# Second batch's pooled loads behind the first batch's x, with a planner that counts 270 GB/s

## The chip, the core and the metric

The kernel runs on one core of a Trainium2 chip. The metric is the device time of one execution in microseconds (us): the median of three runs before the change is 971.7 us (968.58 to 975.79). The engines are named as in the profile: PE is TensorE's matrix product, PEld its weight load, DVE is VectorE, ACT is ScalarE, POOL is GpSimd, and SP is SyncE, which here issues every DMA.

## What is computed

Eight batches of eight heads, 576 positions of 64 elements each. Every head has two attentions whose sum is taken: a pooled one, over groups of four positions (144 pooled positions), and a local one, in which a position sees the three on either side of it. The sum, laid out as 4608 tokens of 512 elements, goes through a feed-forward network (FFN) with 2048 hidden elements and a leaky ReLU.

```python
q_d = q.reshape(B, H, Sd, factor, D).mean(axis=3)          # k_d and v_d likewise, factor = 4
out_up = np.repeat(sm_attn(q_d, k_d, v_d), factor, axis=2)
mask = np.abs(pos[:, None] - pos[None, :]) < factor
scores = np.where(mask, scale * np.matmul(q, k.transpose(0, 1, 3, 2)), -1e9)
attn_out = out_up + np.matmul(softmax(scores), v)
h = x @ w_in                                               # x: attn_out as 4608 x 512
out = np.maximum(0.01 * h, h) @ w_out
```

## The kernel before, in words

The tokens go through the FFN in thirteen chunks: chunks 0 and 1 are the first batch (256 and 320 tokens), then 256, 320 and nine of 384 tokens. Each product in float32 is made of three in a shorter form: x, the hidden values and both weights are each split in a high and a low part (xh and xl, gh and gl, wih and wil, woh and wol). The up product of a chunk and one f (128 hidden elements; f goes from 0 to 15) is twelve matmuls into a bank "hp" (L698); ACT and DVE turn it into gh and gl (L708, L709, L711); the down product is twelve matmuls into four banks acc0 to acc3 (L738). Chunks 0 and 1 go through in two passes each, f 0 to 7 and then f 8 to 15; the second pass loads the stored half output again (L749 to L763) and adds to it. In all this is 4992 matmuls; the texts number them from 0, and chunk 2 begins with number 768.

Weights are made on the chip. `convert(f, k)` loads w_in (k = 0) or w_out (k = 1) of one f into a buffer of 512 KB, copies a part on ACT into a "head" tile (L266), shifts and joins on DVE (L268), casts the high part on ACT or DVE (L279, L276) and subtracts on POOL for the low part (L281). The buffer is free again after the subtraction. For the load it may take any of the buffers k, v, prod (two) and up, and for the first f also xh1 and xl1, which chunk 1 needs later. Weights from f 8 on lie where the first batch's tiles lay, and so are cast only after that batch is done ("late").

The first batch (BANDED = 1) has its local attention on PE (`banded`: scores L453 and L461, transposes L488, value product L502, sums into x at L514 to L521), in two parts: blocks 0 to 3 of 64 positions are chunk 0, blocks 4 to 8 are chunk 1. For the other batches POOL multiplies and DVE adds up: `scores` (L560, L566) loads q and k tiles, `values` (L621, L627) a v tile, and `landing` transposes the result on PE (L658), adds the pooled part and splits it into xh and xl (L665 to L673).

The pooled attention of a batch comes in four units c (two heads each). `pooled` loads q and k as one tile of 576 KB ("qk", one buffer from the second batch on) and v ("vs"), adds groups of four on DVE or POOL (L338, L332, L334), takes scores on PE (L351), the exponential on ACT (L363), transposes (L390) and the value product (L402), and leaves the result in "outd". `widen` repeats it four times in "up" (L645) for the landing.

What runs when is planned while the program is written. Every piece of work is a task with a rank; class `Order` keeps, for each engine, the time at which it is free by its own table of costs (COST, HOP, and a data rate for the DMA wire at L172), and lets the task that can start first write its next instruction. On the chip, each engine then works off its instructions in just that order and waits at each for what it needs. SP does so too: a load behind a store that has nothing to store yet waits with it.

Of the kernel before, what the change touches and what calls it, by code (L numbers as in the profile page):

```python
# [25 lines left out]
NF, NE, NC = DF // 128, DM // 128, DM // 128  # L26
# [2 lines left out]
SIZES = (4, 5, 6, 6, 6, 6, 6, 6, 6, 6, 6)  # L29
QB = 48  # L30
FSPLIT = 8
BANDED = 1
WIN = 64 + W - 1
BLKS = ((0, 4), (4, 9))
# [39 lines left out]
OMAX = max(XMAX)  # L74
COST = {"ACT": (0.13, 0.00083), "DVE": (0.08, 0.00104), "POOL": (0.25, 0.00217)}
HOP = 0.2
SAFE = 0.4
SCARCE, HURRY = ("pt",), 1000

# [16 lines left out]
class Order:  # L96
# [51 lines left out]
    def run(self):  # L148
        while self.tasks:
            for task in sorted((t for t in self.tasks if t[3][0] != "op"), key=lambda t: t[:2]):  # L150
                got = self.grant(task)
                if got is not None:
                    self.resume(task, got)
                    break
            else:
                best = None
                for task in self.tasks:
                    if task[3][0] == "op":
                        _, eng, dur, ready, size = task[3][:5]
                        start = max(self.engine[eng], ready)  # L160
                        if size:
                            start = max(start, self.wire - 6.0)
                        key = (start, task[0], task[1])
                        if best is None or key < best[0]:
                            best = key, task
                assert best is not None, [t[3] for t in self.tasks]
                (start, _, _), task = best
                _, eng, dur, ready, size = task[3][:5]
                free = self.engine[eng]
                self.engine[eng] = start + dur  # L170
                if size:
                    self.wire = max(self.wire, start + 1.2) + size / 300e3  # L172
                    done = self.wire + 0.8
                else:
                    done = start + dur + HOP
                self.log.append((start, eng, dur, task[0], start - free, task[3][5:]))
                self.resume(task, done)
# [3 lines left out]
def attn_moe(ctx: ExitStack, tc, qkt, vd, qb, kb, vb, vwb, band, identb, w_in, w_out, ident, edge, out):  # L181
# [9 lines left out]
    od = Order(bufs)  # L191

    def slot(*tags):
        return (yield ("slot", tags, 0))
# [8 lines left out]
    def op(eng, n, *after, times=1):  # L203
        if eng == "PE":
            dur = n
        else:
            a, k = COST[eng]
            dur = times * a + k * n
        return (yield ("op", eng, dur, max((0.0,) + after), 0, after))
# [9 lines left out]
    def wait(name, n=1):  # L219
        return (yield ("wait", name, n))  # L220
# [30 lines left out]
        nc.vector.memset(h, 0)  # L251

    def convert(f, k):
        s = yield from slot("k", "v", "prod", "up", *(("xh1", "xl1") if f < 4 else ()))
        st = sb(s, [128, HALFS * (DM + 1)], U16)
        raw = st[:, 1:1 + HALFS * DM]
        if k == 0:
            t = yield from load(raw.rearrange("p (c m) -> p c m", c=NC), w_in_v[:, f], 524e3, s.t)
        else:
            t = yield from load(raw, w_out_v[:, f], 524e3, s.t)  # L260
        mid = st.bitcast(I32).rearrange("p (m w) -> p m w", w=2)[:, :DM, 1]
        top = st.rearrange("p (m h) -> p m h", h=HALFS)[:, 1:, 0].bitcast(BF16)
        s_u = yield from slot("head")
        head = heads[s_u.index % len(heads)]
        t = yield from op("ACT", 1500, t, s_u.t)
        nc.scalar.copy(out=head.bitcast(F16).rearrange("p (m h) -> p m h", h=2)[:, :, 1], in_=top)  # L266
        t = yield from op("DVE", 780, t)
        nc.vector.scalar_tensor_tensor(out=mid, in0=mid, scalar=13, in1=head, op0=ALU.logical_shift_right, op1=ALU.bitwise_or)  # L268
        s_u.free(t)
        tf = mid.bitcast(F32)  # L270
        if f >= FSPLIT:
            yield from wait("late")
        hi, lo = (w.rearrange("p c m -> p (c m)") for w in weight(f, k))
        if k:
            t = yield from op("DVE", 512, t)
            nc.vector.tensor_copy(out=hi, in_=tf)  # L276
        else:
            t = yield from op("ACT", 512, t)
            nc.scalar.copy(out=hi, in_=tf)  # L279
        t = yield from op("POOL", 590, t)  # L280
        nc.gpsimd.tensor_tensor(out=lo, in0=tf, in1=hi.bitcast(F32), op=ALU.subtract)  # L281
        s.free(t)
        od.signal(("w", f, k), t)
# [2 lines left out]
    xt = {}  # L286
    kept = {}

    def outd_tile(b):
        s = yield from slot("outd")  # L290
        outd[b] = sb(s, [128, NC, SD], F32)
        od.signal(("outd", b), s.t)
        t = yield from wait(("read", b), 8 if b < BANDED else 2 * len(PARTS[b]))
        s.free(t)
# [11 lines left out]
        s_l.free(t)  # L306

    def fetch(b, c, pool):
        if pool is None:
            sq, sv = (yield from slot(*(("qk", "up") if b < BANDED else ("qk",)))), (yield from slot("vs"))  # L310
            qk, vs = sb(sq, [128, 2, S], F32), sb(sv, [72, 2, 2, D, FAC], F32)
        else:
            sq, sv = None, (yield from slot("su_vs"))
            qk = pool.tile([128, 2, S], F32, name=f"qk{c}")
            vs = sb(sv, [72, 2, 2, D, FAC], F32, pool)
        tq = yield from load(qk, qkt[b, c], 590e3, sq.t if sq else 0.0)
        od.signal(("asked", b, c))
        kept[b, c] = qk
        od.signal(("qk", b, c), tq)
        tv = yield from load(vs, vd[b, c], 295e3, sv.t if sv else 0.0)  # L320
        return sq, sv, qk, vs, tq, tv

    def pooled(b, c, rank, pool=None):
# [4 lines left out]
        if b < BANDED and (b, c) != (0, 0):  # L328
            s = yield from slot("su_half")
# [12 lines left out]
            else:  # L342
                sq.free(t)
        s_st, s_pd = (yield from slot("st_d")), (yield from slot("su_pd" if pool else "pd"))
        s_b = yield from slot(f"acc{c}" if b == 0 else "pt")
        sc = bank(s_b)
        t = yield from pe(0.9, t, s_b.t)
        for qi in range(3):
# [34 lines left out]
        s_pt = yield from slot("su_ptd" if pool else "ptd")  # L383
        ptd = sb(s_pt, [72, 2, 2, 3, QB], F32, pool)
        for kc in range(2):
            s_b = yield from slot("pt")
            tp = bank(s_b)
            tt = yield from pe(0.27, t, s_b.t)
            for qi in range(3):
                nc.tensor.transpose(tp[0:72, qi * 128:(qi + 1) * 128], pd[:, qi, kc * 72:kc * 72 + 72], id_sb)  # L390
            te = yield from op("ACT", 288, tt, s_pt.t)
            nc.scalar.copy(out=ptd[:, kc].rearrange("k p a q -> k a p q"),
                           in_=tp[0:72, :384].rearrange("k (a p q) -> k a p q", a=3, p=2)[:, :, :, :QB])
            s_b.free(te)
        s_pd.free(tt)
        to = yield from wait(("outd", b))
        s_b = yield from slot("pt")
        av = bank(s_b)
        t = yield from pe(0.68, te, td, s_b.t)
        for p in range(2):  # L400
# [26 lines left out]
    def banded(b, c, hf, rank, pool=None):  # L427
# [18 lines left out]
            yield from wait(("wide", b, c))  # L446
            s_pt = shared[b, c]
        s_sm, s_st = (yield from slot("xloc")), (yield from slot("lst"))
        s_b = yield from slot("hp" if (b, hf) == (0, 0) else "pt")
        sp = bank(s_b)  # L450
        spv = sp[:, :nb * WIN].rearrange("p (a k) -> p a k", a=nb)
        t = yield from pe(0.25 + 0.21 * nb, tq, tb, s_b.t)
# [28 lines left out]
        s_st.free(t)  # L481
        pt = wide[b, c][:, b0:b1] if b else sb(s_pt, [WIN, 5, 128], F32, pool)
        for i0, i1 in ((0, 3), (3, nb)):
            s_b = yield from slot("pt")
            tp = bank(s_b)
            tt = yield from pe(0.11 * (i1 - i0), t, s_b.t)
            for i in range(i0, i1):
                nc.tensor.transpose(tp[0:WIN, (i - i0) * 128:(i - i0 + 1) * 128], sm[:, i], id_sb)  # L488
            te = yield from op("ACT", (i1 - i0) * 128, tt, s_pt.t)
            nc.scalar.copy(out=pt[:, i0:i1], in_=tp[0:WIN, :(i1 - i0) * 128].rearrange("k (a q) -> k a q", q=128))  # L490
            s_b.free(te)
# [2 lines left out]
        s_vw, vw = vws[c, hf]  # L494
        to = yield from wait(("pooled", b, c))
        tx = yield from wait(("xbuf", hf))
        s_b = yield from slot(f"acc{c}" if (b, hf) == (0, 0) else "pt")
        av = bank(s_b)
        t = yield from pe(0.21 * nb, te, tv, s_b.t)
        for i in range(nb):  # L500
# [181 lines left out]
    def up_proj():  # L682
        for i, (p, f) in enumerate(steps):
            ch, f0, f1 = PASSES[p]
            n = CHUNKS[ch][1]
            per = 0.012 + n / 2400
            if f == f0:
                tx = yield from wait(("x", ch), LANDED[ch])
            tw = yield from wait(("w", f, 0))
            s_h = yield from slot("hp")  # L690
            hp = bank(s_h)
            xh, xl = xt[ch]
            wh, wl = weight(f, 0)
            k = 0
            for c in range(NC):
                t = yield from op("PE", 3 * per, tx, tw, s_h.t)
                for wt, x in ((wh, xh), (wh, xl), (wl, xh)):
                    nc.tensor.matmul(hp[:, :n], wt[:, c], x[:, c], start=k == 0, stop=k == 3 * NC - 1)  # L698
                    k += 1
            od.spawn(-10, leaky(i, n, s_h, hp, t))  # L700
            if f == f1 - 1:
                od.signal(("done", ch), t)
# [178 lines left out]
```

## Time and profile before

| What | Value |
|---|---|
| median of three runs | 971.7 us (968.58 to 975.79) |
| the profiled execution: its own time, its span | 972.05 us, 970.3 us |
| mean granted clock of PE | 0.98 |
| PE busy | 937.0 us (97%) |
| DVE, ACT, POOL busy | 589.9, 415.0, 610.8 us |
| DMA | 117.31 MB, 121 GB/s over the span |
| first FFN matmul; FFN matmuls in all | at 43.86 us; 4992 |

A busy share is a mean over the whole span, so it is read beside the table of 40 slices, each 24 us long. In the views of instructions a row gives the start in us, the duration in us, engine, line and operation, tiles (out<-in), shape and count, and in brackets the idle time of the engine ahead of it with what ended it. In the list of waits a row gives who waited for whom, the total in us, how often, and the longest. In the chain of work that ended last a row gives start, duration and what ran. In the table of windows the columns are the window, its length, the busy time of the asked engine with its count, the granted clock, the busy share of the DMA engines and GB/s.

### The profile page before, as it was taken

How to read it: one execution, taken by the hardware profiler on the slowest of the kernel's cores; microseconds unless marked ns; L12 is line 12 of the kernel's file. 1: busy time of each engine (PE TensorE's matmuls, PEld its weight loads, DVE VectorE, ACT ScalarE, POOL GpSimd, SP SyncE). 2: the span in 40 equal slices, each digit the busy share in tenths (PEclk: the TensorE clock that was granted, in tenths of full speed). 3: DMA queues.
4: the chain of work that ended last, by engine and by line, in shares of the span. 5: the costliest groups of instructions: out<-in, count | busy, mean ns of one | idle time of the engine just before them, and what ended most of it. 6: DMA issues, size and time to landing. Idle time of an engine off the chain costs nothing.

```text
span 970.3 us, 16161 instructions
## 1 busy us (share of the span) xinstructions
PE 937.0 (97%) x6282; PEld 899.0 (93%) x6282; DVE 589.9 (61%) x895; ACT 415.0 (43%) x1139; POOL 610.8 (63%) x356
## 2 busy tenths in 40 slices
PE   5898998999899999999999999999999999999997
PEld 3697998899799999999999999999999999999997
DVE  4885678867686787678765873873663752411111
ACT  3776664544453454444623543542422523422221
POOL 3574667768788788988889886785695782200000
PEclk9698999999899999999999999999999999999999
DMA  9866756443542544254433543352222311000000
GB/s 254 254 196 191 211 180 190 144 157 113 188 126 83 178 156 125 91 188 149 129 110 92 188 142 103 97 158 82 73 87 94 99 58 50 33 1 1 33 1 33
DMA packets 63180, 117.31 MB, mean 121 GB/s; under 512 B 4944, under 2 KB 32848, under 8 KB 63104
## 3 DMA queue, kind: packets, MB, share of 16 engines
q1 hardware_dynamic: 63104, 116.29, 38.5%
q8 instruction: 49, 0.80, 0.4%
q14 instruction: 27, 0.22, 0.1%
HBM read 105.65 MB, written 10.62 MB: 120 GB/s over the span
## 4 chain that ended last, share of the span: by engine, by line
PE 85%; DMA 8%; POOL 3%; DVE 2%; issue 1%; ACT 1%; SPq 0%; DVEq 0%; POOLq 0%
PE acc L738 39%; PE hp L698 39%; DMA qk<-in_qkt_dram 3%; PE pt L351 2%; PE pt L390 2%; PE pt L402 2%; POOL prod L560 1%; PE pt L658 1%; POOL prod L621 1%; DMA v<-in_w_out_dram 1%; DMA k<-in_kb_dram 1%; DMA su_vw<-in_vwb_dram 1%; DMA v<-in_vb_dram 1%; DMA o<-out_dram 1%; SPq L216 0%
## 5 line engine op out<-in xcount | busy, mean ns | idle before, releaser
L560 POOL TENSOR_TENSOR prod<-q,k 128x1344 f32<-128x1344 f32 (+1 forms) x88 | 260.3, 2959 | 96.9 <-DMA k<-in_kb_dram 66.7
L698 PE MATMUL hp<-xh,wih 128*128 128x384 f32 (+2 forms) x832 | 279.0, 335 | 3.0 <-DVE gl L711 3.0
L621 POOL TENSOR_TENSOR prod<-v,s 128x1344 f32<-128x1344 f32 (+1 forms) x88 | 265.2, 3017 | 24.2 <-DVE xloc L627 16.8
L738 PE MATMUL acc<-gh,woh 128*128 128x384 f32 (+2 forms) x832 | 276.3, 332 | 2.4 <-DVE o L763 2.2
L698 PE MATMUL hp<-xl,wih 128*128 128x384 f32 (+2 forms) x832 | 270.6, 325 | 0.1
L698 PE MATMUL hp<-xh,wil 128*128 128x384 f32 (+2 forms) x832 | 270.7, 325 | 0.0
L738 PE MATMUL acc<-gl,woh 128*128 128x384 f32 (+2 forms) x832 | 269.8, 324 | 0.0
L738 PE MATMUL acc<-gh,wol 128*128 128x384 f32 (+2 forms) x832 | 269.7, 324 | 0.0
L711 DVE TENSOR_TENSOR gl<-hp,gh 128x384 fp32r<-128x384 f32 (+2 forms) x208 | 108.4, 523 | 220.2 <-ACT hp L709 219.4
L708 ACT ACTIVATE gh<-hp 128x384 fp32r<-128x384 f32 (+2 forms) x208 | 97.2, 467 | 335.0 <-PE acc L738 317.2
L698 PEld LDWEIGHTS hp<-xh,wih 128*128 128x128 f32 x832 | 158.1, 190 | 9.7 <-DVE gl L711 4.6
L738 PEld LDWEIGHTS acc<-gh,woh 128*128 128x128 f32 x832 | 156.8, 188 | 7.2 <-issue 4.0
L698 PEld LDWEIGHTS hp<-xl,wih 128*128 128x128 f32 x832 | 158.1, 190 | 0.4 <-DVE xl L521 0.4
L698 PEld LDWEIGHTS hp<-xh,wil 128*128 128x128 f32 x832 | 157.8, 190 | 0.0
L738 PEld LDWEIGHTS acc<-gl,woh 128*128 128x128 f32 x832 | 156.9, 189 | 0.0
L738 PEld LDWEIGHTS acc<-gh,wol 128*128 128x128 f32 x832 | 156.7, 188 | 0.0
L566 DVE TENSOR_REDUCE s<-prod 128x21 f32<-128x1344 f32 (+1 forms) x88 | 130.2, 1480 | 28.0 <-POOL prod L560 28.0
L627 DVE TENSOR_REDUCE xloc<-prod 128x192 f32<-128x1344 f32 (+1 forms) x88 | 130.2, 1480 | 14.0 <-POOL prod L621 13.4
L709 ACT ACTIVATE hp<-hp 128x384 f32<-128x384 f32 (+2 forms) x208 | 96.3, 463 | 0.0
L665 DVE TENSOR_TENSOR pt<-pt,up 128x384 f32<-128x384 f32 (+1 forms) x44 | 37.9, 862 | 34.4 <-PE pt L658 25.9
L645 ACT COPY up<-outd 128x576 f32<-128x576 f32 x84 | 52.3, 675 | 0.0
L363 ACT ACTIVATE pd<-pt,st_d 128x144 f32<-128x144 f32 x84 | 32.0, 381 | 38.3 <-DVE st_d L360 29.0
(114 smaller groups left out, 749.2 us busy)
## 6 DMA issues: line engine op xcount, KB each, us to landing
k<-in_kb_dram SPq DMA_DIRECT2D x38, 576.0 KB
v<-in_vb_dram SPq DMA_DIRECT2D x38, 576.0 KB
qk<-in_qkt_dram SPq DMA_DIRECT2D x32, 576.0 KB
vs<-in_vd_dram SPq DMA_DIRECT2D x28, 288.0 KB
q<-in_qb_dram SPq DMA_DIRECT2D x38, 192.0 KB
out_dram<-o SPq DMA_DIRECT2D x36, 192.0 KB
prod<-in_w_in_dram SPq DMA_DIRECT2D x6, 512.0 KB
prod<-in_w_out_dram SPq DMA_DIRECT2D x6, 512.0 KB
```

Source lines behind the costliest of these rows:

```text
L363: nc.scalar.activation(out=pd[:, qi], in_=scv[:, qi], func=AF.Exp, scale=SCALE / (FAC * FAC), bias=mx[:, qi:qi + 1], accum_out=sm[:, qi:qi ...
L560: nc.gpsimd.tensor_tensor(out=prv, in0=q[:, p, a - j0:z - j0].unsqueeze(2).to_broadcast([128, n, W, D]), in1=view(k[:, p], (a - j0) * D, [ ...
L566: nc.vector.tensor_reduce(out=s[:, p, a - j0:z - j0], in_=prv, axis=AX.X, op=ALU.add)
L621: nc.gpsimd.tensor_tensor(out=prv, in0=view(v[:, p], a - j0, [[1, n], [nv, D], [1, W]]), in1=s[:, p, a - j0:z - j0].unsqueeze(2).to_broadc ...
L627: nc.vector.tensor_reduce(out=xl_t[:, :n, p], in_=prv, axis=AX.X, op=ALU.add)
L645: nc.scalar.copy(out=up[:, pp], in_=outd[b][:, 2 * u + pp].unsqueeze(2).to_broadcast([128, SD, FAC]))
L665: nc.vector.tensor_tensor(out=xv, in0=xv, in1=upv, op=ALU.add)
L698: nc.tensor.matmul(hp[:, :n], wt[:, c], x[:, c], start=k == 0, stop=k == 3 * NC - 1)
L708: nc.scalar.activation(out=gh[:, :n], in_=hp[:, :n], func=AF.Prelu, alpha=0.01)
L709: nc.scalar.activation(out=hp[:, :n], in_=hp[:, :n], func=AF.Prelu, alpha=0.01)
L711: nc.vector.tensor_tensor(out=gl[:, :n], in0=hp[:, :n], in1=gh[:, :n].bitcast(F32), op=ALU.subtract)
L738: nc.tensor.matmul(acc[:, :n], wt[:, es], g[:, :n], start=f == f0 and j == 0, stop=f == f1 - 1 and j == 2)
```

## The change

Four things change. First, a pooled unit of batches 1 to 7 asks for its loads only when the four units of chunk 0's x are written (`wait(("x", 0), NC)`). Second, the planner counts 270 GB/s for the DMA wire in place of 300, and 790 elements for the ACT copy of a weight in place of 1500. Third, the first batch's attention takes any free bank of PSUM (pt, acc0 to acc3, hp) until the first FFN product is written into the plan; before, some products had a bank of their own and the rest shared the two "pt". Fourth, the weights of f 0 to 9 may use k, v, prod and up, and those of f 10 to 15 v, up and vs.

```diff
+OWN = 10
+RATE = 270e3
...
-                    self.wire = max(self.wire, start + 1.2) + size / 300e3
+                    self.wire = max(self.wire, start + 1.2) + size / RATE
...
     def convert(f, k):
-        s = yield from slot("k", "v", "prod", "up", *(("xh1", "xl1") if f < 4 else ()))
+        s = yield from slot(*(("k", "v", "prod", "up") if f < OWN else ("v", "up", "vs")), *(("xh1", "xl1") if f < 4 else ()))
...
-        t = yield from op("ACT", 1500, t, s_u.t)
+        t = yield from op("ACT", 790, t, s_u.t)
...
+    def banks(b):
+        return ("pt", "acc3", "acc2", "acc1", "acc0", "hp") if b == 0 and "started" not in od.events else ("pt",)
...
     def fetch(b, c, pool):
+        if pool is None:
+            yield from wait(("x", 0), NC)
...
     def pooled(b, c, rank, pool=None):
-        s_b = yield from slot(f"acc{c}" if b == 0 else "pt")
+        s_b = yield from slot(*banks(b))
...
-            s_b = yield from slot("pt")
+            s_b = yield from slot(*banks(b))
...
     def banded(b, c, hf, rank, pool=None):
-        s_b = yield from slot("hp" if (b, hf) == (0, 0) else "pt")
+        s_b = yield from slot(*banks(b))
...
-        s_b = yield from slot(f"acc{c}" if (b, hf) == (0, 0) else "pt")
+        s_b = yield from slot(*banks(b))
...
     def up_proj():
             if f == f0:
                 tx = yield from wait(("x", ch), LANDED[ch])
+                od.signal("started")
```

No operation is added or taken away; the order and the buffers change. Line numbers grow: L351 becomes L358, L390 L397, L402 L409, L560 L567, L658 L665, L698 L706, L738 L746. Below are three places of the order, as it is written before and with the change.

SP, ahead of the first FFN matmul, before: the fourth row is batch 1's first load of q and k for the pooled scores, among the first weights (xh, xl, up and k hold weights here; su_vs holds values of the first batch).

```order
L216 DMA up<-in_w_in_dram 128x4x512
L216 DMA xh_102<-in_w_out_dram 128x2048
L216 DMA xl_103<-in_w_in_dram 128x4x512
L216 DMA qk<-in_qkt_dram 128x1152
L216 DMA su_vs<-in_vwb_dram 70x640
L216 DMA vs<-in_vd_dram 72x1024
```

The same place with the change:

```order
L218 DMA xh_102<-in_w_out_dram 128x2048
L218 DMA xl_103<-in_w_in_dram 128x4x512
L218 DMA su_vs<-in_vwb_dram 70x640
L218 DMA vs<-in_w_in_dram 128x4x512
L218 DMA k<-in_w_out_dram 128x2048
```

The pooled loads are gone from here, and the tile vs holds a weight (w_in of f 10).

SP, much later, with the change: the first two of batch 1's pooled loads stand here, after the outputs of chunk 1's first pass begin (128x320) and among the last weights, the reloads of o and the second set of q and k.

```order
L218 DMA vs<-in_w_out_dram 128x2048
L218 DMA up<-in_w_in_dram 128x4x512
L218 DMA out_dram<-o 128x320 x2
L218 DMA qk<-in_qkt_dram 128x1152
L218 DMA v<-in_w_out_dram 128x2048
L218 DMA vs<-in_vd_dram 72x1024
L218 DMA out_dram<-o 128x320 x2
L218 DMA o<-out_dram 128x256
L218 DMA q<-in_qb_dram 128x2x192
L218 DMA k<-in_kb_dram 128x2x576
L218 DMA o<-out_dram 128x256
L218 DMA qk<-in_qkt_dram 128x1152
```

Before, the first of them stood ahead of the FFN and the second among the outputs of chunk 0's first pass (128x256).

PE, before, where 192 FFN matmuls stand ahead: the scores of batch 1's second unit (L351) between the first batch's last value product (L502) and chunk 1's first up product.

```order
L390 MATMUL pt<-id_sb,pd 72x128 x3
L502 MATMUL pt<-su_pt,su_vs 64x64 x10
L351 MATMUL pt<-qk_d 64x144 x6
L390 MATMUL pt<-id_sb,pd 72x128 x3
L698 MATMUL hp<-xh_552,wih_66 128x320
```

PE with the change, where 744 stand ahead: the value product of batch 1's last unit (L409) and the next batch's first scores; 24 down matmuls follow, of which one is shown, then the four last transposes of chunk 2 (L665) and chunk 2's first up product.

```order
L409 MATMUL pt<-ptd,v_d 64x144 x4
L358 MATMUL pt<-qk_d 64x144 x6
L746 MATMUL acc_1769<-gh,woh_951 128x320
...
L665 MATMUL pt<-id_sb,xloc 128x128 x4
L706 MATMUL hp<-xh_1593,wih_66 128x256
```

Counted in the order, the four score products of batch 1 stand behind 0, 192, 387 and 462 FFN matmuls before and behind 492, 558, 612 and 690 with the change; those of batch 2 behind 528 to 714 before and behind 744 to 990 now.

More of the change, by code (lines that the diff above doesn't have):

```diff
@@ L396, in pooled @@
         to = yield from wait(("outd", b))
-        s_b = yield from slot("pt")
+        s_b = yield from slot(*banks(b))
         av = bank(s_b)
@@ L483, in banded @@
         for i0, i1 in ((0, 3), (3, nb)):
-            s_b = yield from slot("pt")
+            s_b = yield from slot(*banks(b))
             tp = bank(s_b)
@@ L496, in banded @@
         tx = yield from wait(("xbuf", hf))
-        s_b = yield from slot(f"acc{c}" if (b, hf) == (0, 0) else "pt")
+        s_b = yield from slot(*banks(b))
         av = bank(s_b)
```

## The prediction

> **What bounds the kernel now.** I read the page first, then TensorE's own waits, then windows around them, and last the queue of SyncE.
>
> ```profile
> span 970.3 us, 16161 instructions
> PE 937.0 (97%) x6282; PEld 899.0 (93%) x6282; DVE 589.9 (61%) x895; ACT 415.0 (43%) x1139; POOL 610.8 (63%) x356
> PE   5898998999899999999999999999999999999997
> PEclk9698999999899999999999999999999999999999
> ...
> PE pt L351 <- DVE qk_d L338: 7.5, 3, 4.1
> PE hp L698 <- DVE gl L711: 3.0, 5, 1.3
> PE acc L738 <- DVE o L763: 2.2, 1, 2.2
> ...
> PE acc L738 <- ACT o L772: 0.3, 1, 0.3
> ```
>
> TensorE is the bound from about 44 us to the end: each slice is 24 us long, and after the eleventh the rows hold nothing but nines. Asked for after 260 us, the waits of TensorE come to the last row alone, 0.3 us. So the change can win only what is lost before 260 us: the start, the waits above, and the half clock that follows them.
>
> ```profile
> 43.86 0.58 PE L698 MATMUL hp<-xh,wih 128*128 128x256 f32 x1
> 82.58 1.71 PE L351 MATMUL pt<-qk_d 64*64 64x144 f32 x12 [4.15 <-DVE qk_d L338]
> 162.37 0.49 PE L738 MATMUL acc<-gh,woh 128*128 128x320 f32 x1 [2.18 <-DVE o L763]
> 252.31 1.71 PE L351 MATMUL pt<-qk_d 64*64 64x144 f32 x12 [2.95 <-DVE qk_d L338]
> ...
> 65.33 3.52 PE acc L738 x30
> 85.07 2.40 PE hp L698 x9
> 100.62 3.52 PE hp L698 x24
> 254.02 3.50 PE hp L698 x12
> ```
>
> The feed-forward product (FFN) starts at 43.86. The lower four rows, from the chain, give its price: 3.52/30 = 0.118 us for 256 columns and 3.52/24 = 0.147 for 320 at full clock, but 2.40/9 = 0.267 and 3.50/12 = 0.29 for 320 just behind a wait. Time behind a wait runs at about half speed, until 87.5 and until 258.1 by the granted clock:
>
> ```profile
> 77.00:88.00 11.00, 6.37 (x53) 0.69 0.71 217
> 159.00:167.00 8.00, 5.82 (x37) 0.79 0.55 149
> 249.00:259.00 10.00, 7.05 (x36) 0.66 0.46 142
> ```
>
> The third number from the right is the clock. A clock of 0.69 over 11 us is 6.8 us at half speed; part of it passes in the wait.
>
> Why the pooled scores (L351) come late is told by their loads:
>
> ```profile
> 76.50 0.45 SPq L216 DMA_DIRECT2D qk<-in_qkt_dram  x1
> ...
> 76.50 4.65 DMA qk<-in_qkt_dram
> 81.17 1.36 DVE qk_d L338
> 241.70 9.09 DMA qk<-in_qkt_dram
> ```
>
> The load for the second unit of batch 1 is issued at 76.50, behind output stores on SyncE, while TensorE's order already has its L351 next.
>
> **(a) The start: -3.5 us.** Ahead of the FFN, VectorE is the narrow engine, and in order:
>
> ```profile
> 23.15 0.69 DVE L268 SCALAR_TENSOR_TENSOR k<-k,head 128x512 int32<-128x512 int32 x1 [2.16 <-ACT head L266]
> 35.42 1.35 DVE L338 TENSOR_REDUCE qk_d<-qk 128x288 f32<-128x1152 f32 x1 [1.82 <-DMA qk<-in_qkt_dram]
> 45.97 0.40 DVE L521 TENSOR_TENSOR xl<-acc,xh 128x256 fp32r<-128x256 f32 x1
> ```
>
> The last of the first chunk's x is written at 45.97 to 46.37. The change takes batch 1's reduce and the wait before it out (1.82 + 1.35), and puts seven ready operations ahead of the first weight, which fills the hole of 2.16: together 5.3. About one comes back, since a further weight shift (0.69) and a softmax sum stand ahead now. TensorE does some window attention before the FFN that used to come behind it (five transposes, ten value products, one score group), which only moves. Bounds: 0, if each closed hole opens the next one, and -5.3; I take -3.5, nearer the holes that I can name.
>
> **(b) The wait at 78 to 88 us: -6.5.** No L351 stands there any more: the first of batch 1 is behind 492 FFN matmuls instead of ahead of all of them, the second behind 558 instead of 192. The idle 4.15 goes, and the half clock from 82.58 to 87.47, 4.9/2 = 2.4. What is next in line there is chunk 1's x, whose last value product stands behind 144 FFN matmuls, and the weights. In the old run the subtraction that ends a weight was never the last wait of TensorE, so I count nothing. Bounds: 0 and -7.
>
> **(c) The pooled units of batch 1, late and close together: +2.5.** They stand behind 492, 558, 612 and 690 matmuls, and chunk 2 starts behind 768. They share one qk buffer, so a unit costs a load and a reduce, 4.65 + 1.36 = 6.0, before the next can load. On TensorE 54 matmuls at 0.118 (256 columns) are 6.4, and with the unit's own products
>
> ```profile
> 108.10 0.33 PE pt L390 x3
> 111.95 0.65 PE pt L402 x8
> 116.43 0.88 PE pt L351 x12
> ...
> 155.26 6.26 DMA o<-out_dram
> ```
>
> 0.88 + 2 x 0.33 + 0.65 = 2.2, that is 8.6 against 6.0: three units are covered. The fourth is not, by my count: on SyncE its load stands behind the stores of pass 2 and the reloads of o, which took 6.26 from issue to landing and cost the 2.18 at 162.37 in the old run. I expect that wait again, about 1 us more at the fourth L351, and 1.5 at chunk 2's first matmul, where the last landing (add, copy, subtract) is now followed by nothing else that could run. Bounds: 0, and +8, if a full wait as at 82.58 (4.15 + 2.4) and the 1.5 come on top.
>
> [...]
>
> **(d) Pooled units of later batches: -4.** The wait of 2.95 at 252.31, with 2.9 behind it, came of the load that took 9.09: it stood behind loads of k and v of 576 KB each.
>
> ```profile
> 239.53 0.60 SPq L216 DMA_DIRECT2D k<-in_kb_dram  x1
> 241.03 0.57 SPq L216 DMA_DIRECT2D v<-in_vb_dram  x1
> ```
>
> The planner that orders the work now counts 270 GB/s instead of 300, and in this stretch the L351s stand 66 to 96 FFN matmuls apart instead of 57 to 72. Ten more matmuls at 0.147 are 1.5 us of cover, twenty 2.9. Bounds: -5.9 and +3, should the same crowd meet another unit; I take two thirds. The copy cost in the planner (790 elements instead of 1500) goes into the same order and is not counted again.
>
> **(e) Three weight buffers for f from 10: 0.** From there the weights may use v, up and vs only, so scores can use k and prod early. What hides it is that the weights are far ahead of their use; the price if not is the first rival.
>
> Sum: -3.5 - 6.5 + 2.5 - 4 = -11.5. The profiled execution took 972.05 (span 970.3 and 1.75 around it), 0.35 over the median of 971.7. So 971.7 - 11.5 = 960.2, say **960 us**.
>
> **Rivals.** A change under 1% (9.7 us) can hardly be told from none.
>
> *Weights starve* (slower). The buffers turn like this:
>
> ```profile
> 84.77 0.38 SPq L216 DMA_DIRECT2D k<-in_w_in_dram  x1
> 95.76 0.33 SPq L216 DMA_DIRECT2D k<-in_w_out_dram  x1
> ...
> 119.34 6.38 POOL L560 TENSOR_TENSOR prod<-q,k 128x896 f32<-128x896 f32 x3
> L268 DVE SCALAR_TENSOR_TENSOR prod<-prod,head x12: 679/694/1795, 32.2 to 110.8; 128x512 int32<-128x512 int32 x12
> ```
>
> A buffer's turn took 11 us. Eleven weights remain for three buffers, so the next to last, w_in of f 15, is ready four turns after the first buffer comes free, which I put at 69.5 (FFN from 42.5, 144 x 0.118 = 17 until chunk 1's last value product, 5 of attention in between and 5 for the first subtractions). TensorE wants it behind matmul 510: 42.5 + 192 x 0.118 + 192 x 0.147 + 126 x 0.118 + 7 of attention is 115 to 116. It decides from a turn of (116 - 69.5)/4 = 11.6 us. With 11, ready at 113.5: just in time. Nine score products at 2.1 now stand among these weights on GpSimd, and two of them in a turn make 15 to 16: with 16 ready at 133.5, 17.5 idle and 2.4 at half clock, 960 + 20 = 980. For it: the margin is thin. Against it: of the old turn the load (4.65 for a larger tile) and the shift (0.69) are half, the rest was mostly queueing, and fewer buffers queue less.
>
> [...]
>
> *The late chain costs it all* (same). (c) at its upper end, +8 instead of +2.5, and (d) at -2: 960 + 7.5 = 968. For it: one buffer and a queue that waits in order. Against: spacing of 8.6 for 6.0.
>
> *All losses go* (faster). With (a) at -4, (b) at -6.5, (c) at 0, (d) at -5.9 and the 2.18 with its half clock of 1.7 gone too, -20.3: 952. For it: a plan nearer to the measured rates should wait less everywhere.
>
> *It does nothing* (same). The waits only change places, since every one saved lets the next unready unit reach TensorE's head sooner: 970. Against: the load at 76.50 was late by position alone.
>
> **How the numbers follow.** Forecast 0.42, its own range 955 to 966; starving 0.10; late chain 0.18; all losses 0.18; nothing 0.12. The range leaves out the upper half of starving and a little at the bottom: 950 to 974. Faster by over 1% (under 962): two thirds of the forecast and all of the 952 case and a little of the late chain, 0.50. Slower by over 1% (over 981): a turn of 16 or more, 0.06. The rest, 0.44, is within 1%.
>
> **What would show it.** The row to compare first, from PE's timeline before:
>
> ```profile
> 188.01 0.38 PE L698 MATMUL hp<-xh,wih 128*128 128x256 f32 x1
> ```
>
> This is chunk 2's first matmul, the 768th of the FFN. Right: the first FFN matmul by 42.5; no wait of TensorE between 70 and 100; clock 1.0 in 77:88; the L351 group (now at L358) waiting under 4 us in all; the 768th FFN matmul at 165 to 172 instead of 188. Wrong: a wait of the FFN up product for a weight subtraction at 110 to 135 (starving), L358 waits of over 3 us each between 110 and 150 (late chain), or a first FFN matmul after 45 us.

## The result, and the profile after

| | before | with the change |
|---|---|---|
| median, us | 971.6 (968.58 to 975.79, 4 runs) | 959.94 (958.19 to 960.46, 4 runs) |
| ratio to before, 95% interval (the medians' own ratio is 0.988) | 1 | 0.9866 (0.9836 to 0.9897) |
| profiled execution: time, span, us | 972.05, 970.3 | 959.72, 957.9 |
| first FFN matmul; the 768th (chunk 2's first), us | 43.86; 188.01 | 44.19; 169.06 |

The page of the changed kernel, its first lines and TensorE's rows of the 40 slices:

```profile
span 957.9 us, 16170 instructions
PE 932.4 (97%) x6282; PEld 894.8 (93%) x6282; DVE 595.2 (62%) x895; ACT 415.0 (43%) x1139; POOL 617.8 (64%) x356
PE   6799999999999999999999999999999999999997
PEclk9899999999999999999999999999999999999999
```

TensorE is as busy as before by share; what went are the eights in its row after the start, and the eights of the clock behind the second slice. TensorE's waits from 45 us on, all of them, with the change:

```profile
PE hp L706 <- DVE gl L719: 5.1, 10, 1.4
PE hp L706 <- ACT xh L678: 0.7, 1, 0.7
PE acc L746 <- ACT o L780: 0.3, 1, 0.3
PE pt L358 <- DVE qk_d L345: 0.3, 1, 0.3
PE hp L706 <- DVE xl L680: 0.3, 1, 0.3
```

Their sum is 6.7 us. Before, the same list held 14.1: the four rows that the prediction shows (7.5, 3.0, 2.2, 0.3) and two waits for ptd, of 0.6 (L390) and 0.5 (L502).

The waits for qk_d and for the reloaded o are gone or nearly so, the waits for gl grew by 2.1. The three windows of the prediction, with the change (length, busy time with its count, clock, DMA share, GB/s):

```profile
77.00:88.00 11.00, 10.00 (x70) 1.00 0.71 227
159.00:167.00 8.00, 8.00 (x67) 1.00 0.36 111
249.00:259.00 10.00, 10.00 (x76) 1.00 0.75 235
```

The clock was 0.69, 0.79 and 0.66 there. The same table for longer stretches, first before, then with the change:

```profile
45.00:135.00 90.00, 84.49 (x727) 0.95 0.64 198
135.00:190.00 55.00, 52.38 (x407) 0.97 0.51 161
190.00:270.00 80.00, 74.39 (x596) 0.96 0.48 150
```

```profile
45.00:135.00 90.00, 85.73 (x719) 1.00 0.61 191
135.00:190.00 55.00, 53.34 (x428) 1.00 0.58 183
190.00:270.00 80.00, 80.00 (x656) 1.00 0.52 167
```

The gain is spread over the first 270 us, and nothing is won behind them. On the contrary: from FFN matmul 2500 to the last the two kernels do the same work, before from 506.01 to 964.95 (458.9 us), with the change from 490.73 to 952.62 (461.9 us).

### The profile page after: what moved, and what is told of

It reads as the page before. It is cut to its first block, busy times and chain, and to the rows that moved or that the text cites. A ratio compares the mean times of both kernels' runs of the same rounds, so it can differ in the third digit from the quotient of the medians.

```text
span 957.9 us, 16170 instructions
## 1 busy us (share of the span) xinstructions
PE 932.4 (97%) x6282; PEld 894.8 (93%) x6282; DVE 595.2 (62%) x895; ACT 415.0 (43%) x1139; POOL 617.8 (64%) x356
## 4 chain that ended last, share of the span: by engine, by line
PE 77%; POOL 8%; DMA 4%; issue 4%; DVE 4%; ACT 2%; SPq 0%; POOLq 0%; DVEq 0%; ACTq 0%
PE hp L706 35%; PE acc L746 34%; POOL prod L567 4%; POOL prod L628 3%; PE pt L358 2%; DMA k<-in_kb_dram 2%; PE pt L397 2%; PE pt L409 2%; PE pt L665 1%; DMA qk<-in_qkt_dram 1%; DVE s L573 1%; DMA v<-in_w_in_dram 0%; SPq L218 0%; DMA vs<-in_w_out_dram 0%; DVE gl L719 0%
## 5 line engine op out<-in xcount | busy, mean ns | idle before, releaser
L567 POOL TENSOR_TENSOR prod<-q,k 128x1344 f32<-128x1344 f32 (+1 forms) x88 | 266.3, 3027 | 81.3 <-DMA k<-in_kb_dram 55.2
L706 PE MATMUL hp<-xh,wih 128*128 128x384 f32 (+2 forms) x832 | 279.9, 336 | 5.8 <-DVE gl L719 5.1
L746 PE MATMUL acc<-gh,woh 128*128 128x384 f32 (+2 forms) x832 | 274.4, 330 | 0.3 <-ACT o L780 0.3
L706 PE MATMUL hp<-xl,wih 128*128 128x384 f32 (+2 forms) x832 | 269.5, 324 | 0.3 <-DVE xl L680 0.3
L706 PE MATMUL hp<-xh,wil 128*128 128x384 f32 (+2 forms) x832 | 269.6, 324 | 0.0
L746 PE MATMUL acc<-gh,wol 128*128 128x384 f32 (+2 forms) x832 | 269.0, 323 | 0.0
L746 PE MATMUL acc<-gl,woh 128*128 128x384 f32 (+2 forms) x832 | 268.9, 323 | 0.0
L706 PEld LDWEIGHTS hp<-xh,wih 128*128 128x128 f32 x832 | 156.4, 188 | 15.6 <-DVE gl L719 8.0
L746 PEld LDWEIGHTS acc<-gh,woh 128*128 128x128 f32 x832 | 156.2, 188 | 4.0 <-issue 3.2
L706 PEld LDWEIGHTS hp<-xl,wih 128*128 128x128 f32 x832 | 156.7, 188 | 0.5 <-DVE xl L680 0.5
L706 PEld LDWEIGHTS hp<-xh,wil 128*128 128x128 f32 x832 | 156.4, 188 | 0.0
L746 PEld LDWEIGHTS acc<-gl,woh 128*128 128x128 f32 x832 | 156.3, 188 | 0.0
L746 PEld LDWEIGHTS acc<-gh,wol 128*128 128x128 f32 x832 | 156.2, 188 | 0.0
```

Of the source, the lines that this page charges most:

```text
L567: nc.gpsimd.tensor_tensor(out=prv, in0=q[:, p, a - j0:z - j0].unsqueeze(2).to_broadcast([128, n, W, D]), in1=view(k[:, p], (a - j0) * D, [ ...
L746: nc.tensor.matmul(acc[:, :n], wt[:, es], g[:, :n], start=f == f0 and j == 0, stop=f == f1 - 1 and j == 2)
```

## The experiments

The written order alone already settles one point: without the first edit (the wait for x) the changed kernel has the same order on all five engines, row for row. The pooled loads are kept back by the fourth edit, in which weights of f 10 to 15 sit in the buffer vs that each pooled unit needs. That was not in the prediction, so the experiments start there. The theories:

- **A**: the slots move the pooled loads, and that move is most of the gain.
- **B, C, D**: the gain is the costs' and banks' (B), the wait's (C); the banks spoil the start (D).

| run | us, median | ratio to before (95%) | first FFN matmul | TensorE idle in 45:135, 135:190, 190:270 | clock there |
|---|---|---|---|---|---|
| before (shown above) | 971.6 | 1 | 43.86 | 5.5, 2.6, 5.6 | 0.95, 0.97, 0.96 |
| the change | 959.94 | 0.9866 (0.9836 to 0.9897) | 44.19 | 4.3, 1.7, 0 | 1.00, 1.00, 1.00 |
| only_slots | 977.25 | 1.0039 (1.0012 to 1.0065) | 41.73 | 4.6, 5.5, 0 | 1.00, 0.94, 1.00 |
| no_slots | 970.42 | 0.9975 (0.9955 to 0.9994) | 42.84 | 2.0, 4.8, 2.5 | 0.96, 0.95, 0.99 |
| only_wait | 975.37 | 1.0017 (0.9990 to 1.0043) | 41.08 | 5.1, 5.6, 3.0 | 0.98, 0.94, 0.98 |
| no_banks | 972.16 | 0.9986 (0.9965 to 1.0006) | 42.90 | 3.5, 6.1, 0.1 | 0.98, 0.91, 1.00 |
| no_wait | 960.32 | 0.9870 (0.9832 to 0.9908) | 44.67 | 4.7, 1.8, 0 | 1.00, 1.00, 1.00 |
| no_rate | 973.26 | 0.9994 (0.9968 to 1.0020) | 41.75 | 5.1, 6.2, 0.9 | 1.00, 0.91, 1.00 |
| rate_275 | 971.36 | 0.9988 (0.9963 to 1.0013) | 44.68 | 2.4, 6.5, 0.3 | 0.98, 0.88, 1.00 |
| own_12 | 969.79 | 0.9966 (0.9943 to 0.9988) | 43.99 | 1.9, 5.9, 2.7 | 0.99, 0.97, 1.00 |
| rate_275_stores | 971.17 | 0.9984 (0.9956 to 1.0012) | 47.07 | 2.6, 6.3, 0.7 | 0.97, 1.00, 1.00 |
| before_stores | 975.29 | 1.0031 (1.0006 to 1.0056) | 44.91 | 2.8, 2.7, 4.2 | 0.94, 1.00, 0.98 |
| change_stores | 968.11 | 0.9958 (0.9932 to 0.9983) | 46.44 | 2.4, 1.3, 0 | 0.97, 1.00, 1.00 |
| change_gap | 958.06 | 0.9854 (0.9826 to 0.9882) | 45.54 | 1.9, 1.3, 0 | 0.99, 1.00, 1.00 |

Idle is the window's length less the busy time. Ratios are to runs of the kernel before on the same chip, whose medians were 971.6 to 973.6. One of the ten executions of no_rate took 5152.0 us, and the record shows no reason; the ratio leaves it out, and the median of the other nine is 973.07.

### Each part alone, and one part undone

**only_slots**, the fourth edit put into the kernel before:

```diff
-        s = yield from slot("k", "v", "prod", "up", *(("xh1", "xl1") if f < 4 else ()))
+        s = yield from slot(*(("k", "v", "prod", "up") if f < OWN else ("v", "up", "vs")), *(("xh1", "xl1") if f < 4 else ()))
```

> The kernel before with the fourth edit alone: weights of f 0 to 9 in k, v, prod and up, those of f 10 to 15 in v, up and vs. In the written order this puts the four score products of batch 1 behind 525, 591, 666 and 714 FFN matmuls in place of 0, 192, 387 and 462; adding the first edit (the wait for x) to it changes no instruction on any engine. Theory A (weights that sit in vs keep the pooled loads back, and that move is most of the gain): 961 to 965 us, no wait for the pooled scores between 70 and 100 us, full clock there. Rival B (the planner's 270 GB/s and the free choice of banks carry the gain, the slots cost nothing and bring nothing, as the prediction put them): 968 to 974 us.

977.25, a little slower than before and outside both ranges. The move is there and the stretch 45 to 135 runs at full clock, but 5.5 us are idle between 135 and 190. A is half right: the slots do move the loads, and that alone is worth nothing.

**no_slots**, the changed kernel with OWN = 16, so that every weight may use the four old slots:

```diff
-OWN = 10
+OWN = 16
```

> The changed kernel with the weights' slots as before (any of k, v, prod, up for every f); wait, 270 GB/s and banks stay. The written order has the four score products of batch 1 behind 45, 186, 285 and 372 FFN matmuls. Theory A: most of the gain is lost, 966 to 972 us, with waits of 3 us or more for pooled scores before 130 us. Rival B: 958 to 963 us.

970.42: without the slots the gain is gone but for 0.25%, as A has it and against B. The expected sign of it is not there: the pooled scores waited 1.3 us in all, and the longest wait is now another one, the transposes of a landing for 4.6:

```profile
PE pt L665 <- DVE st_l L585: 4.6, 1, 4.6
```

The old wait for the second unit is gone here too, although that unit stands behind 186 FFN matmuls, nearly where it stood before (192). Its load was issued at 68.75 in place of 76.50, and TensorE came to its scores at 80.03 without a wait:

```profile
77.00:88.00 11.00, 11.00 (x95) 1.00 0.55 171
```

**only_wait**, the first edit put into the kernel before:

```diff
     def fetch(b, c, pool):
+        if pool is None:
+            yield from wait(("x", 0), NC)
```

> The kernel before with the first edit alone, the wait of the pooled loads for the first chunk's x. The four score products of batch 1 stand behind 48, 195, 258 and 438 FFN matmuls. Theory A: 967 to 974 us, the wait for the second unit is still there. Rival C (the wait itself is the gain, as the change's first line and term (b) of the prediction have it): 961 to 966 us.

975.37, 1.4 above A's range. The wait for the second unit is still there (the clock in 77:88 is 0.84), as A has it; C is out.

**no_banks**, the changed kernel with the banks of before:

```diff
-        s_b = yield from slot(*banks(b))
+        s_b = yield from slot(f"acc{c}" if b == 0 else "pt")
...
-            s_b = yield from slot(*banks(b))
+            s_b = yield from slot("pt")
...
-        s_b = yield from slot(*banks(b))
+        s_b = yield from slot("hp" if (b, hf) == (0, 0) else "pt")
...
-        s_b = yield from slot(*banks(b))
+        s_b = yield from slot(f"acc{c}" if (b, hf) == (0, 0) else "pt")
```

> The changed kernel with the first batch's banks as before. The score products of batch 1 stand behind 486, 570, 645 and 693. Theory A: 959 to 964 us, since the slots and the rate stay. Rival D (any bank is what makes the start wait 2.1 us for xloc and 1.8 us for su_pt, so that the start did not gain its 3.5): the first FFN matmul at 40 to 42 us and 955 to 958 us.

972.16: both sides are out. The slots with the costs give nothing either, and the banks, which looked like a detail of the start, are needed. Here theory A fell. The new one, **E**: no part has a gain of its own. The four together fill the start better and give an order that happens to meet no stall; every other order meets its own.

### Neighbours of the change

**no_wait**, the wait taken out again:

```diff
-        if pool is None:
-            yield from wait(("x", 0), NC)
```

> The changed kernel without the first edit (the wait for x). Every engine's written order is the same as with it, since the slots already keep the pooled loads back. So all theories expect the changed kernel's time: 957 to 963 us, and the trace shows how far two profiled executions of one order differ in their waits and in the steady part from FFN matmul 2500 to the last (461.9 us with the change, 458.9 before). If that part is near 459 here, its 3 us were a matter of the run; if near 462, of the order or the addresses.

960.32, the same time again. The part from matmul 2500 on took 461.6 us, so its 3 us are no matter of one run.

**no_rate**, the planner's two costs as before:

```diff
-RATE = 270e3
+RATE = 300e3
...
-        t = yield from op("ACT", 790, t, s_u.t)
+        t = yield from op("ACT", 1500, t, s_u.t)
```

> The changed kernel with the planner's two costs as before (300 GB/s, 1500 elements); slots, banks and wait stay. 146 other matmul rows' products stand ahead of the first FFN matmul, in place of 172 with the change. Theory E (no part has a gain of its own; two things make it: with costs and banks together 26 more of the first batch's products fit ahead of the FFN, worth 3.5 us, and the plan happens to have no stall between 135 and 190 us, worth some 8): 966 to 973 us. Rival F (banks and slots are enough, the costs bring nothing): 958 to 963 us.

973.26, 0.3 above E's range, but as E has it, and against F.

**rate_275** and **own_12**, one number each:

```diff
-RATE = 270e3
+RATE = 275e3
```

> The changed kernel with 275 GB/s in place of 270. The start is as in the change (172 products ahead of the FFN); from FFN matmul 500 on the order is another one, close to that of the run with the old banks (pooled scores behind 486, 579, 645, 690, 753, 792, 846, 921). Theory E with later stalls drawn anew by each order: 964 to 971 us, the start as good as the change's and new waits between 135 and 190 us. Rival G (the fuller start and an honest rate are the gain, whatever the exact order): 957 to 962 us.

```diff
-OWN = 10
+OWN = 12
```

> The changed kernel with f 0 to 11 in k, v, prod and up, and only f 12 to 15 in v, up and vs. The start is as in the change (172 products); the pooled scores of batch 1 stand behind 486, 540, 630 and 687. Theory E: 960 to 970 us, by the waits that it meets between 135 and 190 us. Rival G: 957 to 962 us.

971.36 (0.4 above E's range) and 969.79. Two per cent more in the planner's rate take the whole gain away, though the order of the start is the change's own in both. In rate_275 the loss is in one stretch; in own_12 most of it is there, and 2.7 us of idle time come between 190 and 270. The rows of 135 to 190, first rate_275, then own_12:

```profile
135.00:190.00 55.00, 48.47 (x338) 0.88 0.60 186
```

```profile
135.00:190.00 55.00, 49.14 (x365) 0.97 0.58 176
```

With the change 53.34 of 55 are busy there at a clock of 1.00. G, by which a better rate helps whatever the order, is out; E stands.

### What makes a stall

In rate_275 the chain of the first stall can be read off. First SyncE's queue, then DVE, then TensorE:

```profile
137.82 0.36 SPq L218 DMA_DIRECT2D out_dram<-o  x1
138.28 0.39 SPq L218 DMA_DIRECT2D qk<-in_qkt_dram  x1
```

```profile
143.42 1.35 DVE L345 TENSOR_REDUCE qk_d<-qk 128x288 f32<-128x1152 f32 x1 [1.69 <-DMA qk<-in_qkt_dram]
144.69 1.11 DVE L672 TENSOR_TENSOR pt<-pt,up 128x256 f32<-128x256 f32 x2
145.71 0.42 DVE L771 TENSOR_TENSOR o<-acc,o 128x256 f32<-128x256 f32 x1
```

```profile
146.19 0.41 PE L746 MATMUL acc<-gh,woh 128*128 128x320 f32 x1 [2.06 <-DVE o L771]
```

The load for the pooled scores is issued behind an output store, DVE has its reduce next and waits, the add that frees a bank stands behind the reduce, and TensorE waits for the bank. It is much like the chain of 82.58 in the kernel before, at another place (there TensorE waited for the reduce itself). With the change the same unit's load was issued at 129.72, ahead of the stores at 136.76.

The other stall, at 177, is one that the neighbours share. In six of the seven kernels above that have no gain (all but no_slots), TensorE waits 1.2 to 3.1 us between 169 and 183, just ahead of chunk 2's first matmul, for the exponential of a pooled unit (L397, in some kernels numbered L395). Only 0 to 15 FFN matmuls stand between that unit's scores and its transposes there; chunk 2's x is not landed yet, and little else could run. With the change the scores stand behind 744, and 33 FFN matmuls follow before the transposes, which do not wait. The first row is rate_275's (scores at 171.88), the second the change's (scores at 164.20):

```profile
177.15 0.30 PE L397 MATMUL pt<-id_sb,pd 128*72 128x128 f32 x1 [1.70 <-ACT pd L382]
```

```profile
171.76 0.38 PE L397 MATMUL pt<-id_sb,pd 128*72 128x128 f32 x2
```

In no_slots TensorE waits 4.59 at the same place for the landing. So E's "every other order meets its own" is too strong: most meet this one. No run moved that unit alone, so this is read from the traces and not tested.

Theory **H** is about the first stall and says that the store ahead of the load is the cause; the next three kernels let ACT issue the stores, all else in its place:

```diff
-        t = yield from load(dest(p, e, n), o[:, :n], 512 * n, t)
+        t = yield ("op", "SP", 0.3, max(0.0, t), 512 * n)
+        nc.scalar.dma_start(out=dest(p, e, n), in_=o[:, :n])
```

> The kernel with 275 GB/s, its output stores issued by ACT in place of SP; nothing else in any engine's order is changed. Theory H (a pooled load waits on SP behind a store whose result is not there yet; DVE and then TensorE wait for it): in the run with 275 GB/s the third load of batch 1's q and k was issued at 138.28, behind a store at 137.82, though its buffer was free at 131.69; DVE idled 1.69 for it, TensorE 2.06 and 1.26 for the add to o that stands behind it, and 6.8 us ran at half clock. All of that goes (some 6.5 us), the wait at 177 (1.7, then half clock) has no store before its load and stays: 963 to 967 us. Rival I (the waits are DVE's own order, or ACT's stores delay ACT by as much): 968 to 974 us.

971.17 against 971.36, in the rival's range and not in H's. DVE no longer waits for this load (its reduce at 144.36 follows without a gap), and no half clock is left behind 50 us: the windows of rate_275 and then of this run:

```profile
147.00:154.00 7.00, 5.74 (x29) 0.53 0.47 149
175.00:185.00 10.00, 7.40 (x37) 0.66 0.85 247
```

```profile
147.00:154.00 7.00, 4.76 (x36) 1.00 0.59 201
175.00:185.00 10.00, 6.46 (x54) 1.00 0.81 242
```

More matmuls fit into each, but the idle time stays (6.3 us in 135 to 190 against 6.5): TensorE still waits 1.69 at 150.83 for the next add to o. By the clock the load is only 0.49 us earlier; but the whole run is some 2.4 us later here (first FFN matmul 47.07 against 44.68), so against its neighbours it is some 2.9 earlier. It now stands behind two loads for the local attention, for whose buffer SyncE had waited since 127.4:

```profile
126.49 0.94 SPq L218 DMA_DIRECT2D vs<-in_vd_dram  x1
136.50 0.55 SPq L218 DMA_DIRECT2D q<-in_qb_dram  x1
137.14 0.56 SPq L218 DMA_DIRECT2D k<-in_kb_dram  x1
137.79 0.55 SPq L218 DMA_DIRECT2D qk<-in_qkt_dram  x1
```

> The kernel before with its output stores issued by ACT in place of SP, all orders otherwise as before. Theory H: the second unit's load of q and k, issued at 76.50 behind the stores of 75.62 though its buffer was free from 37, is issued by 70; the wait of 4.15 at 82.58 and the 2.4 behind it go, the waits at 162 and 252 (no store stands just before the load there) stay: 964 to 968 us. Rival I: no change, 969 to 975 us.

975.29, no gain, and above both ranges. The load that was issued at 76.50 is issued at 70.00, as H has it. But the reduce runs at 80.60 against 81.17, because DVE's order has other operations ahead of it, and the last of these waits for TensorE (the line numbers in these rows are this run's own, five higher than in the kernel before):

```profile
80.20 0.50 DVE L519 TENSOR_TENSOR pt<-pt,outd 128x320 f32<-128x320 f32 x1 [0.93 <-PE pt L507]
80.60 1.34 DVE L343 TENSOR_REDUCE qk_d<-qk 128x288 f32<-128x1152 f32 x1
```

TensorE's wait at this place goes from 4.15 to 1.92, and the clock in 77:88 stays at 0.69:

```profile
82.00 0.50 PE L356 MATMUL pt<-qk_d 64*64 64x144 f32 x2 [1.92 <-DVE qk_d L343]
```

So the store explains 2.2 of the 4.15; DVE's own order, as these rows are read, the rest. H is about half of the cause.

> The changed kernel with its output stores issued by ACT, as a control: no pooled load is late there, so theory H gives nothing to win, and the price of 52 stores on ACT, which is not the bound, is small: 958 to 962 us. Rival I (the stores on ACT cost): 962 to 968 us.

968.11, as rival I has it: 8 us more with the stores on ACT (there are 60 of them, not the 52 of the expectation). One place where they cost shows in ACT's copies into o, with the change and with the stores on ACT; the last numbers are ACT's idle time ahead of them:

```profile
L780 ACT COPY o<-acc 128x384 f32<-128x384 f32 (+2 forms) x50 | 21.6, 458 | 14.0 <-DMA out_dram<-o 8.8 <-PE acc L746 5.2
```

```profile
L780 ACT COPY o<-acc 128x384 f32<-128x384 f32 (+2 forms) x50 | 21.7, 457 | 25.3 <-DMA out_dram<-o 20.1 <-PE acc L746 4.8 <-DMA k<-in_kb_dram 0.4
```

This control gives the two other runs their meaning, if each trace is cut at the first FFN matmul and at number 2500. Between the two, the stores on ACT cost the change 0.5 us (446.5 to 447.0), won 4.6 in rate_275 (455.9 to 451.3) and 2.2 in the kernel before (462.2 to 460.0). From number 2500 on they cost 5.4 (461.9 to 467.3), 2.5 and 0.7. Ahead of the first FFN matmul, where no output store is issued yet, the three executions were 2.3, 2.4 and 1.1 us later, for which the record shows no cause. So what H has in mind is worth some 5 us in rate_275 and 2 to 3 before, and the rest takes it back. The executions are single ones, and the price of issuing on ACT is not the same in the three.

### The steady part

**change_gap**, 32 bytes left free ahead of the weights of f 8 to 15:

```diff
         late = ctx.enter_context(tc.tile_pool(name="late", bufs=1))
+        late.tile([128, 8], F32, name="gap")
```

> The changed kernel with 32 bytes left free ahead of the weights of f 8 to 15, so that these lie 32 bytes higher; every order is the same. In all eight kernels with the new slots or without them, the part from FFN matmul 2500 to the last took 461 to 464 us where those weights lie at byte 162816 of a partition and 459 where they lie at 162784, and in the first the matmuls of f 8 to 15 alone are slower, by 2 to 3 ns each. Theory J (the address decides): that part takes 458 to 460 us and the kernel 955 to 958. Rival K (the address has no part in it): 461 to 463 us there, the kernel 959 to 961.

958.06 is within 0.1 us of J's range and below K's, and the part from matmul 2500 on took 460.9 us, between the two. Worked out from the starts of matmuls that follow each other in chunks 6 to 12 (some 220 of each kind), the down product with gl at f 8 to 15 took 173.1 ns before, 175.9 with the change and 173.4 with the gap; the up product with xl took 173.9, 175.7 and 176.7. With the gap the down product is nearly back at its old spacing, and the up product got slower by another 1.0. So the address moves both, and it explains about 1 us of the 3. The ratio's interval holds the change's own, so this is a version as good as the change; that it is better is not shown.

## Why the prediction was right, and where its steps were not

The time came out as forecast: 959.94 for 960. The terms did not all, and that the total fits this well is luck, as the sum below shows.

**(a) The start, -3.5: right sign, another form.** The first FFN matmul was expected by 42.5 and came at 44.19. The holes on DVE closed, and by as much as forecast: the last of the first chunk's x was written at 42.82 in place of 46.37, 3.55 earlier.

```profile
42.41 0.41 DVE L528 TENSOR_TENSOR xl<-pt,xh 128x256 fp32r<-128x256 f32 x1
```

But the FFN then had TensorE's own work ahead of it (340 matmul rows in place of 306), and TensorE got new waits there:

```profile
PE acc L495 <- POOL xloc L487: 2.1, 1, 2.1
PE acc L397 <- POOL su_pd L378: 2.0, 2, 1.3
PE pt L509 <- ACT su_pt L497: 1.8, 1, 1.8
```

The gain lies in what the prediction called work that "only moves". Of the first batch's window attention, 9.3 us stood behind the first FFN matmul before (3.5, 3.2, 2.0 and 0.6), 6.4 with the change (2.6, 2.4, 1.1 and 0.3); the two largest groups each, before and then with the change:

```profile
L488 PE MATMUL pt<-id_sb,xloc 128*70 128x128 f32 x20 | 3.5, 272 | 0.0
L502 PE MATMUL pt<-su_pt,su_vs 70*64 70x64 f32 x80 | 3.2, 227 | 0.5 <-ACT ptd L392 0.5
```

```profile
L495 PE MATMUL pt<-id_sb,xloc 128*70 128x128 f32 x15 | 2.6, 274 | 0.0
L509 PE MATMUL pt<-su_pt,su_vs 70*64 70x64 f32 x60 | 2.4, 227 | 0.0
```

Less the 0.33 by which the FFN begins later, that is 2.6 won. Batch 1's first score product went the other way (0.9 at full clock), and the first matmuls no longer run at half clock, which is worth 0.42 x 3 = 1.3, before and then with the change:

```profile
44.00:47.00 3.00, 2.94 (x14) 0.58 0.18 71
```

```profile
44.00:47.00 3.00, 3.00 (x33) 1.00 0.03 6
```

That is -3.0 in all. Work moved into idle time is a gain, not a move. The half clock there is a matter of the execution, though: in change_gap, whose order is the same, it lasted until 46.60.

**(b) The wait at 78 to 88, -6.5: right.** No L358 stands there and the clock in 77:88 is 1.00. Which edit did it, the term left open; the change's title names the wait for x, which beside the slots has no effect, while the slots moved the loads. Nor was a move behind 492 matmuls needed: in no_slots the wait went with the unit nearly at its old place. Of the prediction's signs, the one of no wait between 70 and 100 did not hold: 1.7 us of short waits stand there (gl 1.4, o 0.3), for which the term counts nothing.

**(c) Late units of batch 1, +2.5: too high.** Batch 1's L358 did not wait at all, chunk 2's first product waited 1.0 (the rows for xh and xl), and the wait for o with the half clock behind it, 2.18 and some 1.7, is gone. That is about -2.9 in place of +2.5. The step that failed is not the place of the fourth load: it does stand behind stores of pass 2 (136.76, 144.81) and the reloads of o (139.81). It is the step from there to "I expect that wait again, about 1 us more at the fourth L351". The reduce behind that load was over at 152.28, and TensorE came to its scores only at 153.91:

```profile
145.20 0.43 SPq L218 DMA_DIRECT2D qk<-in_qkt_dram  x1
```

```profile
153.91 0.95 PE L358 MATMUL pt<-qk_d 64*64 64x144 f32 x12
```

The third load, at 129.72, stands ahead of those stores. In rate_275 and no_banks, built by nearly the same rules, TensorE waits for o again (3.3 and 3.2 us), so the worry was sound and this order was spared.

**(d) Later units, -4: too low.** The wait at 252.31 and its half clock went whole, -5.9, the bound; the 0.3 that L358 still waits is batch 2's, at 180.91. That is -5.6.

**(e) Slots, 0: wrong as to the part.** They carry the move, as said. The weights were in time: wil of f 15 was done at 116.71, later than the 113.5 of the first rival, and its product began at 122.52, 5.8 us behind:

```profile
115.40 1.31 POOL L283 TENSOR_TENSOR wil<-up,wih 128x512 fp32r<-128x512 f32 x1
```

**Not in the sum**: the waits for gl, +2.1; the steady part, +3.0, of which 0.8 are waits for gl counted already; and the two waits for ptd that went, -1.1. The waits for gl go with the start: in change_gap, with the same order, the first FFN matmul came 1.35 us later, the waits for gl were 2.8 in place of 5.1, and matmul 510 began at 121.71 against 122.52.

With the measured terms the sum is -3.0 - 6.5 - 2.9 - 5.6 + 2.1 + 2.2 - 1.1 = -14.8, and the profiled executions differ by 12.3, so some 2.5 us are in no term. The forecast's -11.5 was near because terms that were missing (+4.3) and terms that were too mild or not there (8.1 in all) partly cancelled, the start's 0.5 beside them, and these 2.5 closed most of the rest. The rivals: starving did not come; "all losses go" describes the first 270 us well, and was kept from 952 in good part by the missing terms. "For it: a plan nearer to the measured rates should wait less everywhere" is refuted by rate_275.

What stays open: whether the place of that one pooled unit is what spares this order between 170 and 190, which was read and not tested; and about half of the 3 us of the steady part (the waits make 0.5 of it, the address about 1).

## What to carry to other kernels

Where a planner writes the order for engines that each work it off in turn, one number in it redraws the whole order, and a gain of 1% may belong to the draw and not to the idea; run neighbours of the number before crediting the idea. Read which edit really moves an instruction from the written order: here the edit that named the wait did nothing beside the others, and the one about buffers did the moving. A late load can have two causes in a row, the queue that issues it and the order of the engine that uses it, and mending one of them uncovers the other: in before_stores the load was issued 6.50 us earlier, and the reduce behind it ran 0.57 earlier.

## What the runs showed of the hardware

**Which waits cost clock.** Waits of 0.96 and 1.81 us within four microseconds left the clock at 1.00 in no_rate, while one of 1.82 in own_12 was followed by half clock. First the wait and the window behind it in no_rate, then in own_12:

```profile
115.42 0.39 PE L706 MATMUL hp<-xh,wih 128*128 128x256 f32 x1 [1.81 <-DVE gl L719]
```

```profile
113.00:118.00 5.00, 3.19 (x25) 1.00 0.94 283
```

```profile
179.65 0.58 PE L706 MATMUL hp<-xh,wih 128*128 128x256 f32 x1 [1.82 <-DVE gl L719]
```

```profile
179.00:183.00 4.00, 3.35 (x16) 0.57 0.84 239
```

The length of a wait alone does not decide. In the granted clock's record the half-clock stretches behind waits are 3.4, 6.8 or 10.2 us long, and its changes lie on a grid of 3.41 us (before: 3.41 from 162.55, 6.83 from 80.63 and from 251.30, and at the start 10.24 from 36.26). Laid on that grid, the 14 traces tell more (idle is time without a matmul row; their ends are modelled). At full clock from 50 us on, TensorE was idle for 1.56 to 3.05 us in 15 of the 16 windows of the grid after which the clock fell. In the 3687 after which it stayed, the idle time was at most 1.55, but for one. The two exceptions had 0.75 (before_stores) and 1.69 (rate_275_stores). The kernel before has three of the falls, after windows with 2.61, 2.18 and 1.94 us idle, and at most 1.28 in the 259 after which its clock stayed; the change has no fall, and at most 1.02 in 263. The waits of no_rate above fall into two windows with 1.24 and 1.53 us idle; in own_12, 1.62 fall into one.

**Spread.** The order of the change took 958.19 to 961.15 us in its eight runs (no_wait among them); before took 967.84 to 981.03. That few waits make a time vary less is not shown: change_stores, whose waits are few too, took 964.93 to 973.86 in ten runs.
